# Attention through memory slots and a routed feed-forward layer: new layout and new issuer for the softmax factors, pieces of 16 tokens

## The chip, the cores and the metric

The kernel runs on one core of one Trainium2 chip. The metric is device time in microseconds (us) of one execution. Shown are the median of three runs of the kernel before and one profiled execution of it.

## The reference

Two blocks follow each other. The inputs q, k and v have the shape 8 batches x 8 heads x 576 tokens x 64; phi has 32 memory slots in the last dimension instead of 64.

```python
a = exp(phi - max(phi, slots)); a = a / (sum(a, slots) + 1e-9)
k_m = einsum('bhsm,bhsd->bhmd', a, k)
v_m = einsum('bhsm,bhsd->bhmd', a, v)
attn = softmax(q @ k_m^T / sqrt(64))          # over the 32 slots
x = (attn @ v_m) -> (8, 576, 512)
scores = x @ w_gate                           # one number a token
for each batch: the 128 tokens of the largest score get
    x + sigmoid(score) * (relu(x @ w1) @ w2)  # w1 512x1024, w2 1024x512
```

All is float32. Which tokens are chosen depends on small differences of scores, which is why the kernel computes the softmax factors and the sums over tokens with split numbers.

## The kernel before, in words

A group is one batch and four of its eight heads; there are 16 groups (`groups`, L110). The program is written as Python generators that a loop (L753 to L786) advances by hand. One pass of the loop is a turn. In each turn the softmaxes advance one step, the splitting of v advances in some turns (L763), the sums over tokens advance 7, 10 or 12 steps of two tokens each (`steps`, L730), the attention of up to two batches advances one step each, and the feed-forward products advance two. This fixes the program order on every engine; each engine then runs its own instructions in that order, and waits for others only through semaphores.

The parts that matter here:

- `softmax` and `keys` (L187, L306) work on one group. Two chains, `ch` 0 and 1, alternate until groups 0 to 7 are done; then chain 0 alone does groups 8 to 15. A group takes about ten steps: some 25 passes of VectorE (DVE) over 128 x 576 elements, with ScalarE (ACT) passes between them. `keys` then transposes the factors on TensorE (PE), copies them to `aS`, splits them into `hi` (12 bits cleared) and `lo` (the remainder), stores both to the DRAM array `aparts` (L323 to L327), and multiplies `aS` with k to get the group's k_m, which two ACT copies put into `kbd` (L336). The buffers of `lo` and `hi` are named "low" and "big"; the next group of the chain writes "lo" and "big" again at L212 and L213. `load_k` (L228) asks for the group's k.
- `split_v` (L284) loads a part of v (L291), splits it on DVE (L294, L296), and stores both parts to the DRAM array `vparts`, each twice (L298). Its pool `vio2` has one buffer in the second half of the program.
- `all_sums` (L355) computes v_m for a set of two batches at a time, so there are four sets of four groups. For each piece of T = 18 tokens `load_rows` (L341) issues five transfers on SyncE's queue (SP): one of `v_rows` and four of `a_rows`, one for each head. Every transfer puts rows of (batch, group, part) on partitions, with the tokens of the piece behind each other in the row, so that one matmul of 32 rows (L382) sums the products of the split parts for one token and one group. There are three buffers of each (`k % 3`), and 576 / 18 = 32 pieces a set. The pieces of a set are not asked for before all four groups were finished 5 turns ago (L367).
- `attention` (L676) centres k_m and v_m, computes `scores`, asks for the q of the next batch (L683, in two halves, two buffers), and goes on with `attend` (L527), `rank` and `gather`; `ffn` (L636) computes the products for the chosen tokens.

All loads go through SP's queue in program order: phi, k, v, q, the weights, and the rows. All stores, and the gathers, are issued by GpSimd (POOL). An issue that waits for a semaphore, for instance for a buffer that is still read, holds up every later issue of its queue.

The layouts of the two DRAM arrays (L830, L831) are

```python
vparts = (B, H // 4, 2, 2, 4, S, Dh)
aparts = (4, B, H // 4, 2, S, 32)       # head first, then batch, group, part, token, slot
```

and `aS`, `hi` and `lo` lie in SBUF as 96 partitions x (6 chunks x 128 columns), where token = chunk * 96 + partition and column = head * 32 + slot.

Of the kernel before, what the change touches and what calls it, by code (L numbers as in the profile page):

```python
# [8 lines left out]
F32 = mybir.dt.float32  # L9
# [11 lines left out]
NC = 6  # L21
# [18 lines left out]
def kernel(  # L40
# [15 lines left out]
    nc = tc.nc  # L56
    ctx.enter_context(tc.manual_schedule())
    B, S, D = out.shape
    PT = S // NC
# [4 lines left out]
    H = 2 * NPR  # L64
    Dh = D // H
    M = P // 4
    F = w1.shape[1]
    KD, KF = D // P, F // P
    SET = 2
    T = 18  # L70
    scale = 1.0 / Dh ** 0.5
    out_flat = out.rearrange("b s d -> (b s) d")

# [15 lines left out]
    vio = first.enter_context(tc.tile_pool(name="vio", bufs=2))  # L89
# [12 lines left out]
    def load_k(i, ch):  # L102
        ks[i] = exs[ch].tile([PT, NC, D // NG], F32, name="kb")
        nc.sync.dma_start(out=ks[i], in_=k[groups[i]])

    def load_q(b, j):
        qs[b, j] = step.tile([P, NPR, S // 2], F32, name="qb")
        nc.sync.dma_start(out=qs[b, j], in_=qT[b, :, :, j * (S // 2):(j + 1) * (S // 2)])
# [78 lines left out]
    def softmax(i, ch):  # L187
# [37 lines left out]
            tt(out=val, in0=end, in1=low, op=ALU.add)  # L225

        yield
        load_k(i, ch)  # L228
        near(den, -0.2734375, ends[0])
        dh = t("dh", I16)  # L230
        act(dh, den, FINE)
# [16 lines left out]
        tt(out=low, in0=low, in1=lo, op=ALU.add)  # L248
        stt(out=num, in0=big, scalar=UP, in1=low, op0=ALU.add, op1=ALU.add)
        yield  # L250

        dl, p = t("lo"), t("big")
        stt(out=dl, in0=den, scalar=FINE, in1=dh, op0=ALU.mult, op1=ALU.subtract)
# [30 lines left out]
    def split_v(some, pool, cuts):  # L284

        n = 4 * S * Dh // P
        for b, g in some:
            for x0 in range(0, n, n // cuts):
                x = slice(x0, x0 + n // cuts)
                vb = pool.tile([P, n // cuts], F32, name="vb")  # L290
                nc.sync.dma_start(out=vb, in_=v[b, g, :, x])  # L291
                yield
                hi = pool.tile([P, n // cuts], F32, name="vhi")
                nc.vector.tensor_single_scalar(hi.bitcast(I32), vb.bitcast(I32), -4096,  # L294
                                               op=ALU.bitwise_and)
                nc.vector.tensor_sub(vb, vb, hi)  # L296
                for vp, src in enumerate((vb, hi)):
                    nc.gpsimd.dma_start(  # L298
                        out=vparts[b, g, :, vp].rearrange("w r s d -> w (r s d)")
                                               .rearrange("w (p x) -> p w x", p=P)[:, :, x],  # L300
                        in_=src.unsqueeze(1).to_broadcast([P, 2, n // cuts]))
                yield
# [3 lines left out]
    def keys(i, ch):  # L306
        ex, (b, g) = exs[ch], groups[i]
        a = soft.pop(i)
        kb = ks.pop(i)
        aS = ex.tile([P, NC * P], F32, name="lo")[:PT].rearrange("p (c m) -> p c m", m=P)  # L310
        for c0 in range(0, NC, 3):
            tp = bank([PT, 3, P])
            for c in range(3):
                nc.tensor.transpose(out=tp[:, c], in_=a[:, (c0 + c) * PT:(c0 + c + 1) * PT],  # L314
                                    identity=ident)
            nc.scalar.activation(aS[:, c0:c0 + 3], tp, AF.Copy)  # L316
        yield
        hi = ex.tile([P, NC * P], F32, name="big")[:PT].rearrange("p (c m) -> p c m", m=P)
        lo = ex.tile([P, NC * P], F32, name="low")[:PT].rearrange("p (c m) -> p c m", m=P)
        nc.vector.tensor_single_scalar(hi.bitcast(I32), aS.bitcast(I32), -4096,  # L320
                                       op=ALU.bitwise_and)
        nc.vector.tensor_sub(lo, aS, hi)  # L322
        for part, src in enumerate((lo, hi)):  # L323
            for h in range(4):
                nc.gpsimd.dma_start(  # L325
                    out=aparts[h, b, g, part].rearrange("(c p) m -> p c m", p=PT),
                    in_=src[:, :, h * M:(h + 1) * M])  # L327
        km = bank([P, 2, 2 * M])
        for rr in range(2):
            for c in range(NC):  # L330
                nc.tensor.matmul(out=km[:, rr], lhsT=kb[:, c, rr * P:(rr + 1) * P],  # L331
                                 rhs=aS[:, c, rr * 2 * M:(rr + 1) * 2 * M],
                                 start=(c == 0), stop=(c == NC - 1))
        for u in range(2):
            part = slice(u * Dh, (u + 1) * Dh)
            nc.scalar.activation(kbd[b][part, 2 * g:2 * g + 2, u * M:(u + 1) * M],  # L336
                                 km[part, :, u * M:(u + 1) * M], AF.Copy)

    accs = [accp.tile([P, 512], F32, name=f"acc{i}") for i in range(2 * SET)]

    def load_rows(k, st, ch):  # L341

        some = slice(st * SET, (st + 1) * SET)
        nc.sync.dma_start(
            out=v_rows[k % 3][0::2].rearrange("p s d -> p (s d)").bitcast(F32),
            in_=vparts[some].rearrange("b g t w r s d -> (b g t w r) (s d)")
                [:, ch * T * Dh:(ch + 1) * T * Dh])
        for h in range(4):
            src = aparts[h, some].rearrange("b g t s m -> (b g t) (s m)")
            src = src[:, ch * T * M:(ch + 1) * T * M]  # L350
            nc.sync.dma_start(  # L351
                out=a_rows[k % 3][2 * h::8, h].rearrange("p s m -> p (s m)").bitcast(F32),
                in_=src.unsqueeze(1).to_broadcast([4 * SET, 2, T * M]))

    def all_sums():  # L355
# [7 lines left out]
        def load_some(end):  # L363
            while len(loaded) < min(end, len(pieces)):
                st, ch = pieces[len(loaded)]

                if not all(turn >= made.get(i, turn) + 5  # L367
                           for i in range(st * SET * NG, (st + 1) * SET * NG)):
                    break
                load_rows(len(loaded), st, ch)  # L370
                loaded.append(turn)
# [155 lines left out]
    def attend(b, general):  # L527
        eT, tg = eTs[b % 2], tgs[b % 3]
        row, rest = mean[b]
        for c0 in range(0, NT, 2):  # L530
# [5 lines left out]
                                     rhs=heads_of, start=True, stop=True)  # L536
            if working:
                yield
            rd = step.tile([P, 2, H], F32, name="rd")[:, :cols]
            nc.vector.tensor_scalar(out=rd.rearrange("p c (g h) -> p c g h", g=2), in0=den,  # L540
                                    scalar1=float(M), scalar2=1e-9, op0=ALU.add, op1=ALU.add)
# [134 lines left out]
    def attention(b, general=False):  # L676
        yield from centre(b)
        yield
        yield from (scores_less_max if general else scores)(b)
        for j in range(2):  # L680
            yield
            if not general and b + 1 < B:
                load_q(b + 1, j)  # L683
        yield from attend(b, general)
        yield
        yield from rank(b)
        for t in range(nt):
            yield from gather(b, t)
            chosen.append((b, t))
# [62 lines left out]
    turn = 0  # L752
    while True:  # L753
# [6 lines left out]
        if working and next(working[0], working) is working:  # L760
            finish(working[1])
            working.clear()
        if working and turn % (2 if attend_all else 4) == 1:  # L763
            next(working[1], None)
        for _ in range(steps()):
            next(sums, None)
        if attend_all is None and set(order[1]) <= set(made):
# [4 lines left out]
                ctx.enter_context(tc.tile_pool(name=name, bufs=2 - (name == "one"),  # L772
                                               reuse_waits="tile"))
                for name in ("step", "work", "one"))
            vio = ctx.enter_context(tc.tile_pool(name="vio2", bufs=1, reuse_waits="tile"))
            working[1] = split_v(groups[two + 1:], vio, 2)
            for j in range(2):
                load_q(0, j)
# [58 lines left out]
```

## Time and profile before

| what | value |
|---|---|
| median of three runs | 908.98 us (899.76 to 917.44) |
| profiled execution, its own time | 899.93 us |
| its span | 898.1 us, 25253 instructions |
| mean granted TensorE clock | 0.822 |
| PE busy (PE weight loads) | 584.2 us (427.7) |
| DVE busy | 611.5 us |
| ACT busy | 295.3 us |
| POOL busy | 234.9 us |
| stores of `aparts`, issued by POOL | 64 of `lo`, 46.9 us; 64 of `hi`, 46.5 us; 72 KB each |
| stores of `vparts`, issued by POOL | 23 and 23, 16.9 and 16.6 us; 1152 or 576 KB each |
| row loads, issued by SP | 128 of `v_rows`, 288 KB each; 512 of `a_rows`, 36 KB each |

Line 2 of the page gives the busy share in 40 slices of 22.5 us, in tenths:

```profile
PE   0122322556764646695847889867889989888794
DVE  4899888857874765779789685979845333537820
ACT  3434434324441513332433624343331310332130
POOL 7033311330220432151423314232511010112200
DMA  6367936876857786788554778664256566123300
```

The first sum over tokens starts at 142.6 us and the last at 772.8 us; the last store of softmax factors is issued at 649.7 us. A line of a list of waits reads: the engine and the line that waited, what it waited for, us in total, how often, and the longest. "SPq" is SyncE's queue of transfers. A line of a list in order of time has the start, the duration, the engine, the line, the operation, destination <- source and how many of them.

### The profile page before, as it was taken

To read this page: it belongs to the slowest core of one execution; us is meant where nothing else is said; L and a number is where in the kernel's file an instruction comes from. 1 tells how busy PE (TensorE), PEld (TensorE's weight loads), DVE (VectorE), ACT (ScalarE), POOL (GpSimd) and SP (SyncE) were. 2 spreads that over 40 slices of the span, in tenths; PEclk is the share of its full clock that TensorE was granted. 3 is DMA by queue.
4 is the path that set the end of the run, shared out by engine and by line. 5 is a ranking of instruction groups with operands and counts; after the bars stand their busy time and mean duration, and the time that the engine had idled before them with its cause. 6 is when DMAs were issued, how large, how long until landed. Compare 5 with 4: busy or idle time off the path is not lost. (4 is left out here: it accounts for less than half of the span.)

```text
span 898.1 us, 25253 instructions
## 1 busy us (share of the span) xinstructions
PE 584.2 (65%) x10738; PEld 427.7 (48%) x10738; DVE 611.5 (68%) x1117; ACT 295.3 (33%) x578; POOL 234.9 (26%) x349
## 2 busy tenths in 40 slices
PE   0122322556764646695847889867889989888794
PEld 0012222456653535574714557555556577544441
DVE  4899888857874765779789685979845333537820
ACT  3434434324441513332433624343331310332130
POOL 7033311330220432151423314232511010112200
PEclk9999999757585776886667979985899977989597
DMA  6367936876857786788554778664256566123300
GB/s 169 144 198 271 312 124 204 274 250 176 253 154 241 231 259 186 254 289 254 181 186 139 221 210 256 201 191 138 71 171 195 181 202 204 58 77 117 117 25 15
DMA packets 61944, 166.10 MB, mean 185 GB/s; under 512 B 11136, under 2 KB 21376, under 8 KB 61824
## 3 DMA queue, kind: packets, MB, share of 16 engines
q1 hardware_dynamic: 40096, 94.14, 34.8%
q0 software_dynamic: 21728, 70.27, 23.7%
q8 instruction: 87, 1.43, 0.7%
q14 instruction: 33, 0.27, 0.1%
HBM read 96.21 MB, written 68.16 MB: 183 GB/s over the span
## 5 line engine op out<-in xcount | busy, mean ns | idle before, releaser
L382 PE MATMUL acc<-a_rows,v_rows 32*64 32x128 f32 x9216 | 214.3, 253 | 127.8 <-DMA a_rows<-aparts 121.4
L382 PEld LDWEIGHTS acc<-a_rows,v_rows 32*64 32x64 f32 x9216 | 193.5, 162 | 170.4 <-issue 83.0
L314 PE MATMUL bank<-ident,num 128*96 128x128 f32 x96 | 21.3, 386 | 104.4 <-DVE num L279 99.4
L331 PE MATMUL bank<-lo,kb 96*128 96x64 f32 x384 | 64.5, 345 | 20.0 <-ACT lo L316 20.0
L331 PEld LDWEIGHTS bank<-lo,kb 96*128 96x128 f32 x384 | 62.7, 257 | 25.5 <-ACT lo L316 22.4
L325 POOL DMA_DIRECT2D aparts<-low x64 | 46.9, 740 | 104.8 <-DVE low L322 89.7
L298 POOL DMA_DIRECT2D vparts<-vb x23 | 16.9, 735 | 217.8 <-DVE vb L296 217.8
L654 PE MATMUL bank<-w_sb,xeT 128*128 128x512 f32 x128 | 69.8, 679 | 4.9 <-ACT xeT L645 3.2
L314 PEld LDWEIGHTS bank<-ident,num 128*96 128x96 f32 x96 | 15.4, 178 | 108.8 <-issue 88.4
L664 PE MATMUL bank<-w_sb,hT 128*128 128x512 f32 x128 | 60.8, 609 | 0.0
L548 PE MATMUL bank<-vbd,eT 128*128 128x256 f32 x160 | 58.3, 499 | 0.0
L552 DVE TENSOR_TENSOR xj<-bank,rd 128x512 f32<-128x512 f32 x40 | 27.5, 688 | 32.9 <-PE bank L548 32.4
L601 DVE SCALAR_TENSOR_TENSOR cmp<-row,tg,wide 128x576 bf16<-128x576 f32 x40 | 32.5, 814 | 24.0 <-ACT row L587 23.1
L325 POOL DMA_DIRECT2D aparts<-big x64 | 46.5, 734 | 3.8 <-DMA vparts<-vhi 3.7
L548 PEld LDWEIGHTS bank<-vbd,eT 128*128 128x128 f32 x160 | 34.1, 236 | 16.0 <-issue 12.1
L654 PEld LDWEIGHTS bank<-w_sb,xeT 128*128 128x128 f32 x128 | 25.3, 215 | 30.6 <-issue 22.1
L275 ACT ACTIVATE vh<-num,sm 128x576 f16<-128x576 f32 x16 | 12.4, 776 | 78.2 <-DVE sm L270 63.1
L555 POOL TENSOR_TENSOR xj<-xj,mean 128x1024 f32<-128x1024 f32 (+1 forms) x11 | 23.6, 2147 | 49.5 <-DVE xj L552 41.6
L479 DVE SCALAR_TENSOR_TENSOR eT<-es,th 128x288 f32<-128x288 f32 x32 | 14.4, 450 | 31.9 <-ACT th L477 31.9
L664 PEld LDWEIGHTS bank<-w_sb,hT 128*128 128x128 f32 x128 | 22.5, 189 | 25.9 <-issue 24.4
L336 ACT ACTIVATE kbd<-bank 64x64 f32<-64x64 f32 x32 | 7.0, 218 | 83.5 <-PE bank L331 83.3
L560 POOL DMA_DIRECT2D out<-xj x24 | 16.3, 678 | 66.8 <-DVE xj L555 63.8
(149 smaller groups left out, 1155.8 us busy)
## 6 DMA issues: line engine op xcount, KB each, us to landing
v_rows<-vparts SPq DMA_DIRECT2D x128, 288.0 KB
a_rows<-aparts SPq DMA_DIRECT2D x512, 36.0 KB
vparts<-vb POOLq DMA_DIRECT2D x9, 1152.0 KB, 5.5
vparts<-vhi POOLq DMA_DIRECT2D x9, 1152.0 KB, 8.7
kb<-in_k SPq DMA_DIRECT2D x16, 576.0 KB
qb<-in_qT SPq DMA_DIRECT2D x16, 576.0 KB
out<-xj POOLq DMA_DIRECT2D x16, 512.0 KB, 4.1
xs<-xj POOLq DMA_DIRECT2D x16, 512.0 KB, 4.3
```

Of the source, the lines that this page charges most:

```text
L298: nc.gpsimd.dma_start(out=vparts[b, g, :, vp].rearrange("w r s d -> w (r s d)") .rearrange("w (p x) -> p w x", p=P)[:, :, x], in_=src.unsq ...
L314: nc.tensor.transpose(out=tp[:, c], in_=a[:, (c0 + c) * PT:(c0 + c + 1) * PT], identity=ident)
L325: nc.gpsimd.dma_start(out=aparts[h, b, g, part].rearrange("(c p) m -> p c m", p=PT), in_=src[:, :, h * M:(h + 1) * M])
L331: nc.tensor.matmul(out=km[:, rr], lhsT=kb[:, c, rr * P:(rr + 1) * P], rhs=aS[:, c, rr * 2 * M:(rr + 1) * 2 * M], start=(c == 0), stop=(c = ...
L382: nc.tensor.matmul(out=accs[i][:Dh, :P].rearrange("p (h m) -> p h m", m=M), lhsT=vr[p, s], rhs=ar[p, :, s], start=(ch == 0 and s == 0), st ...
L548: nc.tensor.matmul(out=o[:, g * 4 * Dh:(g + 1) * 4 * Dh], lhsT=eT[:, g, (c0 + c) * P:(c0 + c + 1) * P], rhs=vbd[b % 3][:, g], start=False, ...
L552: nc.vector.tensor_mul(x[:, c].rearrange("p (h d) -> p h d", d=Dh), o.rearrange("p (h d) -> p h d", d=Dh), rd[:, c].unsqueeze(2).to_broadc ...
L555: (nc.gpsimd if working else nc.vector).tensor_add(x, x, row.unsqueeze(1).to_broadcast([P, cols, D]))
L560: nc.gpsimd.dma_start(out=out[b, c0 * P:c0 * P + (cols - 1) * P + n].rearrange("(c p) d -> p c d", p=n), in_=x[:n])
L601: nc.vector.scalar_tensor_tensor(out=cmp, in0=row, scalar=g, in1=wide[:, off:off + S], op0=ALU.is_equal, op1=ALU.mult, accum_out=equal[:, ...
L654: nc.tensor.matmul(out=ps[:n], lhsT=xeT[:, d, :n], rhs=w1_sb[:, d, f0:f0 + 512], start=(d == 0), stop=(d == KD - 1))
L664: nc.tensor.matmul(out=ps[:n], lhsT=hT[:, f, :n], rhs=w2_sb[:, f], start=(f == 0), stop=(f == KF - 1))
```

## The change

T becomes 16, so that a set has 36 pieces, and `aparts` gets the layout (batch, group, part, chunk, head, 96 tokens, slot). In it 16 tokens of one head lie behind each other, since 16 divides 96. The eight stores a group by POOL become two by ACT, one for each part, behind the k_m copies. The stores of v's parts move from POOL to ACT too, one step after DVE's subtraction. The smaller row buffers leave room for a second buffer in `vio2`. `load_k` moves one step later in `softmax`, `load_q` from `attention` into the first round of `attend`. The pieces of a set may be asked for 4 turns after its groups instead of 5, and `split_v`, which now has three steps a part instead of two, advances in one turn of three (before: four) and later in two of three (before: one of two).

```diff
--- before.py
+++ after.py
@@ -67,7 +67,8 @@
     F = w1.shape[1]
     KD, KF = D // P, F // P
     SET = 2
-    T = 18
+    T = 16
+    assert PT % T == 0
     scale = 1.0 / Dh ** 0.5
     out_flat = out.rearrange("b s d -> (b s) d")
 
@@ -225,7 +226,6 @@
             tt(out=val, in0=end, in1=low, op=ALU.add)
 
         yield
-        load_k(i, ch)
         near(den, -0.2734375, ends[0])
         dh = t("dh", I16)
         act(dh, den, FINE)
@@ -248,6 +248,7 @@
         tt(out=low, in0=low, in1=lo, op=ALU.add)
         stt(out=num, in0=big, scalar=UP, in1=low, op0=ALU.add, op1=ALU.add)
         yield
+        load_k(i, ch)
 
         dl, p = t("lo"), t("big")
         stt(out=dl, in0=den, scalar=FINE, in1=dh, op0=ALU.mult, op1=ALU.subtract)
@@ -294,8 +295,9 @@
                 nc.vector.tensor_single_scalar(hi.bitcast(I32), vb.bitcast(I32), -4096,
                                                op=ALU.bitwise_and)
                 nc.vector.tensor_sub(vb, vb, hi)
+                yield
                 for vp, src in enumerate((vb, hi)):
-                    nc.gpsimd.dma_start(
+                    nc.scalar.dma_start(
                         out=vparts[b, g, :, vp].rearrange("w r s d -> w (r s d)")
                                                .rearrange("w (p x) -> p w x", p=P)[:, :, x],
                         in_=src.unsqueeze(1).to_broadcast([P, 2, n // cuts]))
@@ -320,11 +322,6 @@
         nc.vector.tensor_single_scalar(hi.bitcast(I32), aS.bitcast(I32), -4096,
                                        op=ALU.bitwise_and)
         nc.vector.tensor_sub(lo, aS, hi)
-        for part, src in enumerate((lo, hi)):
-            for h in range(4):
-                nc.gpsimd.dma_start(
-                    out=aparts[h, b, g, part].rearrange("(c p) m -> p c m", p=PT),
-                    in_=src[:, :, h * M:(h + 1) * M])
         km = bank([P, 2, 2 * M])
         for rr in range(2):
             for c in range(NC):
@@ -335,6 +332,10 @@
             part = slice(u * Dh, (u + 1) * Dh)
             nc.scalar.activation(kbd[b][part, 2 * g:2 * g + 2, u * M:(u + 1) * M],
                                  km[part, :, u * M:(u + 1) * M], AF.Copy)
+        for part, src in enumerate((lo, hi)):
+            nc.scalar.dma_start(
+                out=aparts[b, g, part].rearrange("c h p m -> p (c h) m"),
+                in_=src.rearrange("p c (h m) -> p (c h) m", m=M))
 
     accs = [accp.tile([P, 512], F32, name=f"acc{i}") for i in range(2 * SET)]
 
@@ -346,8 +347,8 @@
             in_=vparts[some].rearrange("b g t w r s d -> (b g t w r) (s d)")
                 [:, ch * T * Dh:(ch + 1) * T * Dh])
         for h in range(4):
-            src = aparts[h, some].rearrange("b g t s m -> (b g t) (s m)")
-            src = src[:, ch * T * M:(ch + 1) * T * M]
+            src = aparts[some, :, :, ch * T // PT, h].rearrange("b g t p m -> (b g t) (p m)")
+            src = src[:, ch * T % PT * M:(ch * T % PT + T) * M]
             nc.sync.dma_start(
                 out=a_rows[k % 3][2 * h::8, h].rearrange("p s m -> p (s m)").bitcast(F32),
                 in_=src.unsqueeze(1).to_broadcast([4 * SET, 2, T * M]))
@@ -364,7 +365,7 @@
             while len(loaded) < min(end, len(pieces)):
                 st, ch = pieces[len(loaded)]
 
-                if not all(turn >= made.get(i, turn) + 5
+                if not all(turn >= made.get(i, turn) + 4
                            for i in range(st * SET * NG, (st + 1) * SET * NG)):
                     break
                 load_rows(len(loaded), st, ch)
@@ -536,6 +537,9 @@
                                      rhs=heads_of, start=True, stop=True)
             if working:
                 yield
+            if c0 == 0 and not general and b + 1 < B:
+                for j in range(2):
+                    load_q(b + 1, j)
             rd = step.tile([P, 2, H], F32, name="rd")[:, :cols]
             nc.vector.tensor_scalar(out=rd.rearrange("p c (g h) -> p c g h", g=2), in0=den,
                                     scalar1=float(M), scalar2=1e-9, op0=ALU.add, op1=ALU.add)
@@ -679,8 +683,6 @@
         yield from (scores_less_max if general else scores)(b)
         for j in range(2):
             yield
-            if not general and b + 1 < B:
-                load_q(b + 1, j)
         yield from attend(b, general)
         yield
         yield from rank(b)
@@ -760,7 +762,7 @@
         if working and next(working[0], working) is working:
             finish(working[1])
             working.clear()
-        if working and turn % (2 if attend_all else 4) == 1:
+        if working and (turn % 3 if attend_all else turn % 3 == 1):
             next(working[1], None)
         for _ in range(steps()):
             next(sums, None)
@@ -772,7 +774,7 @@
                 ctx.enter_context(tc.tile_pool(name=name, bufs=2 - (name == "one"),
                                                reuse_waits="tile"))
                 for name in ("step", "work", "one"))
-            vio = ctx.enter_context(tc.tile_pool(name="vio2", bufs=1, reuse_waits="tile"))
+            vio = ctx.enter_context(tc.tile_pool(name="vio2", bufs=2, reuse_waits="tile"))
             working[1] = split_v(groups[two + 1:], vio, 2)
             for j in range(2):
                 load_q(0, j)
@@ -828,7 +830,7 @@
                                    kind="ExternalInput").ap())
     out = nc.dram_tensor("out", (B, S, H * Dh), F32, kind="ExternalOutput").ap()
     vparts = nc.dram_tensor("vparts", (B, H // 4, 2, 2, 4, S, Dh), F32, kind="Internal").ap()
-    aparts = nc.dram_tensor("aparts", (4, B, H // 4, 2, S, phi.shape[3]), F32, kind="Internal").ap()
+    aparts = nc.dram_tensor("aparts", (B, H // 4, 2, NC, 4, PT, phi.shape[3]), F32, kind="Internal").ap()
     xs = [nc.dram_tensor(f"xs{b}", (S, H * Dh), F32, kind="Internal").ap() for b in range(B)]
     with tile.TileContext(nc) as tc:
         tile_abc_attention__then__mixture_of_depths_kernel(tc, *args, out, xs, vparts, aparts, int(moe_capacity))
```

## The prediction

> **What bounds the kernel now.** I read the page's slices first, then the waits of the whole span, then the SP queue in order of time, and last the busy times of stretches cut where the row loads start and stop. The program splits into five stretches: softmaxes alone (0 to 138 us), the sums of sets 0 and 1 (138 to 420), a pause (420 to 460), the sums of set 2 beside softmaxes and attention (460 to 650, the last 40 of them idle for the sums), the sums of set 3 (650 to 773), and the rest (773 to 898).
>
> ```profile
> core 0: us, PE busy (x) PEld busy (x) DVE busy (x) ACT busy (x) POOL busy (x), PEclk, DMA share, GB/s
> 138.00:266.00 128.00, 72.87 (x2136) 66.89 (x2136) 100.48 (x159) 48.29 (x78) 29.28 (x42) 0.73 0.73 225
> 266.00:420.00 154.00, 96.48 (x2664) 81.16 (x2668) 105.03 (x192) 46.82 (x90) 43.44 (x59) 0.72 0.76 238
> 460.00:611.00 151.00, 116.53 (x2481) 81.05 (x2483) 120.69 (x223) 58.61 (x115) 49.43 (x62) 0.86 0.68 206
> 651.00:773.00 122.00, 113.32 (x2550) 79.51 (x2546) 49.99 (x105) 22.81 (x56) 15.25 (x25) 0.89 0.61 186
> ```
>
> These lines come from one table of stretches each. From 138 to 420 no compute engine is full: DVE has 205.5 of 282 us, PE 169. From 460 on DVE (120.7 of 151) and then PE (113.3 of 122) are near their limit. So 138 to 420 is bound by something else. The waits of PE between 200 and 300 us and the SP queue in order of time name it:
>
> ```profile
> PE acc L382 <- DMA a_rows<-aparts: 32.4, 13, 8.6
> ```
>
> ```profile
> 211.87 0.50 SPq L344 DMA_DIRECT2D v_rows<-vparts  x1
> 212.41 2.45 SPq L351 DMA_DIRECT2D a_rows<-aparts  x4
> 214.96 0.50 SPq L344 DMA_DIRECT2D v_rows<-vparts  x1
> 215.51 2.44 SPq L351 DMA_DIRECT2D a_rows<-aparts  x4
> 218.05 0.50 SPq L344 DMA_DIRECT2D v_rows<-vparts  x1
> 218.60 2.45 SPq L351 DMA_DIRECT2D a_rows<-aparts  x4
> 221.14 0.50 SPq L344 DMA_DIRECT2D v_rows<-vparts  x1
> 221.69 4.99 SPq L351 DMA_DIRECT2D a_rows<-aparts  x4
> ```
>
> SP issues without a pause: one piece of 18 tokens takes 3.09 us from start to start, five issues and nothing else, and PE waits for what they bring. Adding all SP lines from 137.5 to 420.3 gives 245.6 us of issuing in 282.8: 257 a_rows issues took 186.2 us (148.8 at the usual 579 ns) and 63 v_rows issues 43.8 (31.6 at 502 ns). So 50 us are stretched issues, like the 4.99 above. The remaining 37 us are mostly gaps of 0.05 to 0.1 us between issues, and some 20 us of SP waiting for a free row buffer (L344 on PE acc). I take this stretch as bound by SP's issuing. PE works in order, so its stalls hold the transposes of the softmaxes back too.
>
> The queue's own waits over the whole span are what the change aims at:
>
> ```profile
> SPq L291 <- DMA vparts<-vb: 105.0, 6, 28.3
> ...
> SPq L351 <- DMA aparts<-big: 67.1, 6, 38.9
> SPq L344 <- PE acc L382: 62.7, 37, 11.6
> SPq L108 <- PE bank L490: 29.7, 2, 25.2
> SPq L104 <- PE bank L331: 21.8, 4, 13.7
> ```
>
> Asked by stretches of 100 us, they lie badly for a gain: of the 105.0 us of L291, 53.4 fall before 100 us (no rows are loaded then), 17.4 in 100 to 200 and 34.2 in 420 to 460; the 25.2 of L108 fall after the last row load, and only 4.6 of L104's between 138 and 420.
>
> **The Trainium skill.** "Perfetto Trace Analysis", section "DMA Instruction — HWDGE (DVE, Sync)", says that the block that generates descriptors is shared by the two issuing sequencers and locked for one of them at a time, and that the profiled time of an issue includes the wait for the lock. Here only SP issues that way, so the trace cannot confirm the sharing; that issue time grows from 0.58 to 2.9 us at worst agrees that more than decoding is in it. "DMA: Bandwidth & Descriptors", section "Issuing engines are not separate DMA queues", says that transfers started by any engine run on the same 16 engines, so that another issuer saves sequencer time only. The trace agrees in so far as SP's long issues start beside POOL's large stores: 221.69 follows the two vparts stores at 221.12 and 221.83, 144.34 those at 143.01 and 143.71.
>
> **The change part by part.** The sum is against the profiled execution, 899.9 us (span 898.1); the median of the runs shown is 909.0, so 9 us are added at the end.
>
> 1. *Pieces of 16.* 576/16 = 36 pieces a set instead of 32; each is still five SP issues, of the same forms with shorter rows, so 3.09 us undisturbed. Sets 0 and 1: 8 more pieces, 8 x 3.09 = +25 us, all of it on the bound. Set 3 (650 to 773): +12.4 us of issuing; SP has 122.6 - 104.7 = 18 us free there, about 9 of them gaps that cannot be filled, so +4. Set 2 (460 to 611): 150.6 - 114.4 = 36 us free, 26 after gaps, which covers +12.4 (it would cost that whole without the slack); +2 for more PE stalls. Bytes are unchanged. Together +31.
>
> 2. *Factors stored by ACT.* POOL loses 128 issues (46.9 + 46.5 us) and 46 for v (16.9 + 16.6). ACT gains 32 + 46. ACT's issue price is not in the trace. A store is now 96 x 24 = 2304 pieces of 128 bytes. Lower bound: SP's cheapest issue, 0.33 us. Upper: POOL gives off 576 such pieces each 0.74 us without a growing delay to landing (3.5 and 4.3 us), so the DMA engines take them at least that fast: 4 x 0.73 = 2.9 us. Nearest rows: qb, 512 rows in 0.59 us, and w2, 1024 rows in 1.16: 1.14 ns a row, 2.6 us for 2304. I take 2.6. For v's parts (256 rows) 0.5 us. ACT thus gets 32 x 2.6 + 46 x 0.5 = 106 us on top of 295; it has room over the span. What matters is whether those issues keep SP from its own. From 138 to 420 there are 7 groups and 12 v pieces: 14 x 2.6 + 24 x 0.5 = 48 us of ACT issuing. If the block is locked, up to +48 us; if not, 0. Part falls where SP waits for a buffer or is stretched by busy DMA engines anyway, so I take +15. Set 2's stretch: 4 groups, 5 v pieces, 26 us against 14 of slack left: 0 to +12, I take +4.
>
> 3. *Order on ACT.* The store now stands behind the kbd copies (L336), so it waits for nothing itself. Behind it in ACT's queue stand the next group's activations and the attention's es and th; each is held 5.2 us at most. The next group's lo and big (L212, L213) must wait until the store has read them: before, ACT waited 0.2 us for this. Issue 5.2 plus landing 4 against two turns of some 4.8 us: 0 to 3 us a group, 16 groups; I take +5 in all. v's parts get a yield between DVE's subtraction and the issue, so ACT shouldn't wait for DVE there.
>
> 4. *Waits taken from SP.* Second vio2 buffer: the 21 us block at 438.6 to 460.0 ends earlier, so set 2 starts up to 13 us earlier (its last factors were issued by 442.7 and landed some 4 us later). But set 2 ends at 611 and set 3's rows wait until 650.4 for the last softmax, so that is mostly hidden; it moves some PE work ahead: -5. k one step later: -4 (the 4.6 us above). q later: L108's 25.2 us have no row loads behind them, 0; q now comes in attend, about one turn before the next batch's scores instead of two or three, a danger of -0/+5, taken as 0. One turn less after a softmax (5 to 4): at sets 0 and 3 SP already stands waiting for factors (26.3 and 38.9 us), so 0.
>
> 5. *POOL freed.* POOL's addition (L555) no longer stands behind 5.8 us of issues; DVE waited for it 6.7 us in all: -4. v's slower pace (a piece per 9 turns for 8, then 4.5 for 4) is still ahead of the sums: 0.
>
> Sum: 31 + 15 + 4 + 5 - 5 - 4 - 4 = +42: 942 us, by the median 951. Since the free bounds of 2 and 3 reach further down than I put them, I forecast 947.
>
> **Rivals.**
>
> *A, faster: the stretch goes away.* The 50 us of stretched issues between 138 and 420 come when POOL throws two stores of up to 1152 KB into the DMA engines within 1.4 us. Issued by ACT and a step later, they may be served in turn with the rows. Without the stretch and without contention: 899.9 + 31 - 13 - 50 = 868, 877 by the median. It decides from the point where more than 31 - 13 = 18 us of the 50 are saved, and beats 2% from 36. For it: the coincidences at 144 and 221 us. Against: the bytes and the DMA engines are the same.
>
> *B, no change: the stores cost SP nothing*, and the earlier start of set 2 is worth its whole 13 us: 899.9 + 31 - 21 = 910, 919 by the median. For it: the lock shows in no line. Against: nothing then explains a gain beyond that.
>
> *C, much slower: the lock holds in full*, and lo and big wait 2 us a group: 899.9 + 31 + 48 + 12 + 32 - 13 = 1010, 1019 by the median. For it: the skill's wording and SP's 87% use. Against: ACT has idle time, and the 26 us pieces of stage 460 to 611 may fall in pauses.
>
> **How the numbers follow.** Chances: the forecast 0.48 (its own range 927 to 975), A 0.27 (865 to 891), B 0.17 (891 to 927), C 0.08 (975 to 1025). Faster by over 2%, which is about what a measurement can tell from no change, is A: 0.27; within 2% is B: 0.17; slower is the forecast and C: 0.56. The range leaves out A's lower end and C: 873 to 978.
>
> **What would show it.** Right: v_rows x144 and a_rows x576 at about 502 and 579 ns, a piece at 3.09 us; sets 0 and 1 taking over 300 us from the first a_rows to the last; PE's wait for a_rows well above 121 us; ACT's aparts issues near 2.6 us. Wrong: row issues much shorter than 579 ns; the stretched part gone while ACT stores; ACT's issues near 0.4 us; or a softmax stage (to the last aparts store, now at 650) that is shorter than before.

## The result, and the profile after

The changed kernel takes 1013.2 us (median of 4 runs, 1011.7 to 1014.5) against 905.9 for the kernel before in the same comparison: a ratio of 1.121, 95% interval 1.113 to 1.129. It is slower, and by more than the range of the prediction (873 to 978) allowed. The profiled execution took 1011.9 us (span 1010.1), 112 us more than that of before.

These stretches of after answer to those shown of before, cut by the same rule: from the first to the last issue of `a_rows` of a set, and for set 3 to the last sum. Sets 0 and 1 now run from 145 to 493, set 2 from 519 to 699, set 3 from 745 to 883:

```profile
core 0: us, PE busy (x) PEld busy (x) DVE busy (x) ACT busy (x) POOL busy (x), PEclk, DMA share, GB/s
145.00:312.00 167.00, 82.33 (x2168) 76.19 (x2168) 102.15 (x161) 49.48 (x80) 0.41 (x2) 0.62 0.61 187
312.00:493.00 181.00, 108.72 (x2684) 90.72 (x2685) 107.15 (x196) 46.11 (x89) 13.82 (x20) 0.63 0.64 194
519.00:699.00 180.00, 134.06 (x2564) 92.43 (x2563) 125.12 (x234) 63.12 (x122) 28.23 (x31) 0.78 0.62 186
745.00:883.00 138.00, 118.38 (x2553) 81.14 (x2549) 50.02 (x105) 22.83 (x56) 14.63 (x23) 0.86 0.52 162
```

Sets 0 and 1 take 348 us instead of 282, with nearly the same DVE work (209 us, before 205.5). Set 2 takes 180 instead of 150 (its first `a_rows` was issued at 461 before), set 3 takes 138 instead of 122. These are 112 us. What lies around them adds up to nothing: the row loads start 7 us later, the pause ahead of set 2 is 15 us shorter, the one ahead of set 3 is 6 us longer, and what follows the last sum is 2 us longer (127.7 us, before 125.3). So the loss lies in the stretches in which rows are loaded. The bytes are the same and the share of the DMA engines' time in use fell, so the engines are no fuller than before. PE's wait between 200 and 300 us:

```profile
PE acc L383 <- DMA a_rows<-aparts: 55.7, 13, 16.1
```

It was 32.4 us; over the span it is 203.7 (before 121.4). The granted clock fell too, from 0.822 to 0.767, and PE's busy time in sets 0 and 1 rose by 22 us. Had a slower PE held SP back, SP's wait for a row buffer that PE still reads would have grown; it is 62.0 us, before 62.7. But no run holds the clock fixed, so a part of the time, in set 3 above all (PE 118.4 us, before 113.3), may be the clock's.

The waits of SP's queue over the span hold what is new:

```profile
SPq L352 <- DMA aparts<-big: 92.5, 6, 46.2
...
SPq L345 <- PE acc L383: 62.0, 35, 13.8
SPq L292 <- DMA vparts<-vb: 42.3, 4, 14.8
SPq L105 <- PE bank L328: 41.6, 3, 16.7
SPq L109 <- PE bank L491: 30.1, 2, 25.7
SPq L352 <- DMA vparts<-vb: 28.9, 5, 13.5
SPq L345 <- DMA vparts<-vb: 26.7, 5, 11.4
SPq L352 <- DMA vparts<-vhi: 16.8, 11, 3.8
```

The last three lines are loads of rows (L345, L352) that wait for stores of v's parts. With a line of 3.0 us for L345 and vparts<-vhi they sum to 75.4 us. The kernel before has 1.3 us of it (its L351 is L352 here):

```profile
SPq L351 <- DMA vparts<-vb: 0.7, 1, 0.7
SPq L351 <- DMA vparts<-vhi: 0.6, 1, 0.6
```

L352 reads `aparts` and needs nothing from `vparts`. Two lists in order of time show one such place, SP's queue first, ACT's issues second:

```profile
161.82 2.45 SPq L352 DMA_DIRECT2D a_rows<-aparts  x4
164.37 0.50 SPq L345 DMA_DIRECT2D v_rows<-vparts  x1
170.59 4.08 SPq L352 DMA_DIRECT2D a_rows<-aparts  x4
174.76 0.50 SPq L345 DMA_DIRECT2D v_rows<-vparts  x1
```

```profile
164.72 0.37 ACTq L300 DMA_DIRECT2D vparts<-vb  x1
165.12 0.53 ACTq L300 DMA_DIRECT2D vparts<-vhi  x1
171.91 0.33 ACTq L336 DMA_DIRECT2D aparts<-low  x1
172.28 2.31 ACTq L336 DMA_DIRECT2D aparts<-big  x1
```

SP stands from 164.87 to 170.59, until the store that ACT issues at 164.72 has landed. Why it must is in the program: the transfers issued by SP and by ACT take turns on eight semaphores in program order, and each waits until the last transfer on its semaphore has landed. The trace agrees: the load at 170.59 waits for the very semaphore that the store at 164.72 carries, and all 872 transfers of SP and ACT in it use the same eight. These are five consecutive transfers of SP's program; the number behind DMAHW names the semaphore, 0 to 7:

```
L352 DMACopy a_rows0_106<-aparts 16x1x512 [waits DMAHW4_49]
L352 DMACopy a_rows0_106<-aparts 16x1x512 [waits DMAHW5_49]
L352 DMACopy a_rows0_106<-aparts 16x1x512 [waits DMAHW6_49]
L345 DMACopy v_rows1_104<-vparts 64x1024 [waits DMAHW1_49,PE_49]
L352 DMACopy a_rows1_107<-aparts 16x1x512 [waits DMAHW2_49]
```

Between 6 and 1, the numbers 7 and 0 have gone to two transfers of ACT. In the kernel before only SP's transfers took numbers of this set, and the next one waited for SP's own transfer eight back, mostly landed; POOL's have another eight. Now SP, which runs far ahead of the compute engines, can pass a transfer of ACT's by seven places and no further. ACT reaches it in its own order, behind DVE.

### The profile page after: what moved, and what is told of

Its sections match the earlier page's. It is cut to its first block, busy times and chain, and to the rows that moved or that the text cites. A ratio compares the mean times of both kernels' runs of the same rounds, so it can differ in the third digit from the quotient of the medians.

```text
span 1010.1 us, 25145 instructions
## 1 busy us (share of the span) xinstructions
PE 624.2 (62%) x10738; PEld 456.6 (45%) x10738; DVE 610.9 (60%) x1116; ACT 295.2 (29%) x578; POOL 108.6 (11%) x176
## 3 DMA queue, kind: packets, MB, share of 16 engines
q10 hardware_dynamic: 86752, 47.19, 16.4%
## 5 line engine op out<-in xcount | busy, mean ns | idle before, releaser
L383 PE MATMUL acc<-a_rows,v_rows 32*64 32x128 f32 x9216 | 228.1, 263 | 209.4 <-DMA a_rows<-aparts 203.7
L383 PEld LDWEIGHTS acc<-a_rows,v_rows 32*64 32x64 f32 x9216 | 206.0, 172 | 255.6 <-issue 152.3
L316 PE MATMUL bank<-ident,num 128*96 128x128 f32 x96 | 21.7, 391 | 105.9 <-DVE num L280 105.9
L328 PE MATMUL bank<-lo,kb 96*128 96x64 f32 x384 | 68.7, 360 | 19.7 <-ACT lo L318 17.9
L658 PE MATMUL bank<-w_sb,xeT 128*128 128x512 f32 x128 | 75.6, 728 | 5.1 <-ACT xeT L649 4.3
L328 PEld LDWEIGHTS bank<-lo,kb 96*128 96x128 f32 x384 | 66.9, 272 | 24.1 <-ACT lo L318 19.8
L322 DVE TENSOR_SCALAR big<-lo 96x768 int32<-96x768 int32 x16 | 8.8, 552 | 55.4 <-ACT lo L318 55.4
L245 DVE SCALAR_TENSOR_TENSOR lo<-num,vh 128x576 f32<-128x576 f32 x16 | 12.1, 755 | 41.0 <-ACT vh L182 41.0
L205 DVE SCALAR_TENSOR_TENSOR ph<-q,ph 128x576 f32<-128x576 int16 x32 | 25.4, 795 | 17.6 <-ACT q L182 17.1
L318 ACT ACTIVATE lo<-bank 96x384 f32<-96x384 f32 x32 | 14.5, 483 | 65.8 <-PE bank L316 65.7
L536 PEld LDWEIGHTS bank<-heads_of,eT 128*128 128x128 f32 x160 | 29.8, 270 | 5.1 <-issue 3.0
```

The source lines that it names most:

```text
L205: stt(out=r, in0=q, scalar=-ln2, in1=r, op0=ALU.mult, op1=ALU.add)
L383: nc.tensor.matmul(out=accs[i][:Dh, :P].rearrange("p (h m) -> p h m", m=M), lhsT=vr[p, s], rhs=ar[p, :, s], start=(ch == 0 and s == 0), st ...
L536: nc.tensor.matmul(out=den[:, c, g], lhsT=eT[:, g, (c0 + c) * P:(c0 + c + 1) * P], rhs=heads_of, start=True, stop=True)
L658: nc.tensor.matmul(out=ps[:n], lhsT=xeT[:, d, :n], rhs=w1_sb[:, d, f0:f0 + 512], start=(d == 0), stop=(d == KD - 1))
```

## The experiments

Three theories were set against each other. Theory 1: the shared semaphores tie SP to ACT. Theory 2: the busy path, that is the bytes, the 128-byte pieces and the long issues on the way through ACT. Theory 3: the additional issues of T = 16. Six of the kernels make a path from before to after, on which each step is one edit or one group of edits. Times are medians, and "before" was 905.9 to 911.4 us in the comparisons. The intervals reach about 4 to 7 us to each side, so a step of a few us cannot be told from nothing.

| kernel | us | ratio to before, 95% interval | PE waits for a_rows, us |
|---|---|---|---|
| before | 909 | | 121.4 |
| T = 16 alone | 948.2 | 1.043, 1.038 to 1.048 | 142.6 |
| and the edits of order | 935.3 | 1.029, 1.022 to 1.037 | 151.6 |
| and the new layout, two stores by POOL | 953.3 | 1.045, 1.038 to 1.052 | 166.3 |
| and the second vio2 buffer | 954.2 | 1.051, 1.046 to 1.055 | 166.1 |
| and v's parts stored by ACT | 995.2 | 1.098, 1.092 to 1.103 | 194.4 |
| and the factors stored by ACT (after) | 1013.2 | 1.121, 1.113 to 1.129 | 203.7 |

The steps are +39, -13, +18, +1, +41 and +18 us.

**T = 16 alone.**

```diff
-    T = 18
+    T = 16
```

> The kernel before with T = 16 and nothing else. Theory 1 (shared slots: SP's row loads wait for ACT's late stores, because the transfers that SP and ACT issue take turns on eight semaphores): T = 16 is only a part, 31 us as in the forecast, so 930 to 940 us. Theory 2 (busy path: ACT's stores of 128-byte pieces load the DMA engines and stretch SP's issues): the same, 930 to 940. Theory 3 (SP's issue time for the 16 additional pieces is the main cost and was underrated): 970 us or more.

Measured: 948.2 us, +38 over 910.3 in its comparison. A bit more than the term of the forecast (31), far from theory 3's 970. Its profile is of a run of 953.7 us, 54 above the profile of before. There sets 0 and 1 take 24 us more, as the forecast had it (25), but set 2 takes 11 more (forecast 2) and set 3 takes 145 us instead of 122, where the forecast had 4 more.

**Stores by POOL, in the new layout.** The changed kernel with this edit at both places, v's parts and the factors:

```diff
-                    nc.scalar.dma_start(
+                    nc.gpsimd.dma_start(
```

> The changed kernel, but all stores of factors and of v's parts issued by POOL again, in the new layout and at the new places. Theory 1: POOL's transfers have semaphores of their own, so the waits of SP for stores go and the time falls to 930 to 945 us. Theory 2: falls as far, if POOL's stores are packed into fewer packets as before. Theory 3: stays at 990 us or more.

Measured: 954.2 us, ratio 1.051 (1.046 to 1.055): the issuer is worth 59 us, and theory 3 falls as the main cause. Theory 1 had 945 at most; it left out the merging of the stores, which costs 17 us (below). The place and the size of the stores are as in the changed kernel, and POOL's transfers take none of the eight semaphores; SP's row loads wait 2.4 us for vparts stores.

**One of the two kinds of store by POOL.** The same edit for v's parts only, and for the factors only.

> The changed kernel, but v's parts stored by POOL again; the factors are still stored by ACT. Theory 1: in the changed kernel SP waits 75 us for vparts stores that its loads don't need, against few for the factors beyond the 92 us that are mostly a true dependence; without them 950 to 975 us. Theory 2: the 128-byte pieces remain, so 995 us or more.

> The changed kernel, but the factors stored by POOL, in two transfers a group; v's parts are still stored by ACT. Theory 1: the waits for vparts stores remain, 975 us or more. Theory 2: the 128-byte pieces leave the hardware path, 950 us or less.

Measured: 973.4 us (1.063 to 1.078) with v's parts back on POOL, 995.2 (1.092 to 1.103) with the factors back on POOL. Both as theory 1 had it; v's parts are the dearer half.

**Small transfers by ACT.** The kernel before, with `note()` behind each store of v's parts and twice behind the k_m copies:

```diff
+    def note():
+        nc.scalar.dma_start(out=notes[len(noted)], in_=ident[:16, :64])
+        noted.append(1)
...
+                    note()
```

> The kernel before, plus 78 small transfers (16 rows of 256 bytes from a constant to a scratch array) issued by ACT where the changed kernel's ACT issues stand: two behind each group's k_m copies, two behind each v part. They wait for no data, carry next to no bytes and few descriptors, and nobody reads them. Theory 1 (shared slots): each takes one of the eight semaphores that SP's loads use in turn, so SP stands until ACT has come to it: 945 to 970 us, with SP waits for these transfers in the trace. Theory 2 (busy path: bytes, packets and long issues): 915 us or less.

Measured: 929.3 us, ratio 1.022 (1.014 to 1.030). SP's row loads wait 18.1 us for the small transfers. Theory 1 is seen nearly without bytes, but smaller than expected (945 to 970); theory 2 expected 915 or less. It stayed open what carries the rest.

**Long pieces.** The changed kernel with each store of 96 pieces of 3072 bytes; it leaves out that the factors must lie in the order in which the row loads read them. Number, size and addresses of the row loads stay the same:

```diff
-                out=aparts[b, g, part].rearrange("c h p m -> p (c h) m"),
-                in_=src.rearrange("p c (h m) -> p (c h) m", m=M))
+                out=aparts[b, g, part].rearrange("c h p m -> (c h p m)").rearrange("(p x) -> p x", p=PT),
+                in_=src.rearrange("p c k -> p (c k)"))
```

> The changed kernel, but each factor store writes 96 pieces of 3072 bytes instead of 2304 of 128: the factors are laid down partition by partition, which is not the order in which the row loads read them, so this run leaves the right order of the factors out. Theory 1: the number of stores and what they wait for are the same, so 1000 us or more. Theory 2: the cost of 128-byte pieces goes, about the 18 us between the run with v by ACT and the changed kernel, or more: 995 us or less.

Measured: 987.2 us, ratio 1.085 (1.078 to 1.091), 26 us below the changed kernel. Here theory 2 was right: for the factors it is the pieces that cost. With long pieces the kernel is even 8 us below the one with the factors stored by POOL (995.2). ACT's issues of the two stores, min, median and max in ns, first in the changed kernel, then with long pieces:

```profile
L336 ACTq DMA_DIRECT2D aparts<-low x16: 311/329/340, 48.4 to 739.4; - x16
L336 ACTq DMA_DIRECT2D aparts<-big x16: 1986/2252/4621, 48.7 to 739.7; - x16
```

```profile
L336 ACTq DMA_DIRECT2D aparts<-low x16: 310/328/341, 48.3 to 710.4; - x16
L336 ACTq DMA_DIRECT2D aparts<-big x16: 437/440/711, 48.7 to 710.8; - x16
```

The first store is issued in 0.33 us in both; the second takes 2.25 us in the changed kernel, against 0.44. The Trainium skill, "DMA: Bandwidth & Descriptors", section "Specifications", has 512 bytes as the least piece for full rate; these runs agree in direction: for the same bytes ACT's stores take 13.0% of the DMA engines' time over a span of 984.6 us with long pieces, against 16.4% over 1010.1, which is 128 against 166 us.

How the pieces cost time is seen on ACT itself. The word "issue" stands for idle time in which an engine waited for nothing that the profile shows. In the changed kernel each of these times follows directly on a store's issue by ACT; first the changed kernel, then long pieces:

```profile
ACT dh L182 <- issue: 20.2, 6, 4.8
ACT ph L200 <- issue: 6.8, 2, 4.7
```

```profile
ACT ph L200 <- issue: 3.1, 3, 2.0
ACT dh L182 <- issue: 1.1, 2, 0.6
```

L182 and L200 are activations of the softmaxes, which stand behind the store issues in ACT's program order. With long pieces the first `a_rows` is issued at 134.6 us instead of 145.0, so 10 of the 26 us are gained before any row is loaded. How the rest divides between these waits and the busier DMA engines was not tried apart. The row loads still wait 53 and 17 us for v's stores here, so the pieces and the shared semaphores are two separate causes.

**The edits of order alone**, on the kernel before, T = 18, stores by POOL: `load_k` and `load_q` later, 4 turns for 5, the additional yield and the pace of `split_v`.

> The kernel before with only the edits of order: k and q asked for later, pieces 4 turns after a group, the additional step in splitting v and its new pace. T stays 18, stores stay with POOL, one vio2 buffer. From the run with POOL's stores less the run with T = 16 alone (954 less 948) I expect 905 to 920 us; if the edits of order cost by themselves and the second buffer and the new layout paid them back, 925 or more.

Measured: 898.9 us, ratio 0.987 (0.976 to 0.998). This part of the change seems to gain: the interval hardly leaves 1 out, but the same edits also gain 13 us at T = 16 (948.2 to 935.3). It is the only version here whose time lies below both kernels.

**Fewer and larger pieces, and the reverse.** To test that the count of issues is what T costs, T = 24 with two row buffers (`k % 2`, `load_some(k + 2)`) and T = 12 with four (`k % 4`, `load_some(k + 4)`), otherwise the kernel before:

```diff
-    T = 18
+    T = 24
```

> The kernel before with T = 24 and two row buffers instead of three: 24 pieces a set, so five issues for 24 tokens. If SP's issue time bounds the stretch from 138 to 420 us, 40 issues fewer a set give back what T = 16 cost: 870 to 890 us. If the number of buffers matters as much (48 tokens in flight instead of 54, and only one piece ahead), 906 us or more.

```diff
-    T = 18
+    T = 12
```

> The kernel before with T = 12 and four row buffers: the same 48 tokens in flight as with T = 16 and three, but 48 pieces a set instead of 36. If the count of SP's issues is what T = 16 pays for, 24 more pieces in sets 0 and 1 at 3.09 us cost 74 us over the run with T = 16 alone, and more in the last set: 1010 us or more. If the tokens in flight are what it pays for, about as T = 16: 940 to 960 us.

Measured: T = 24 took 940.1 us, ratio 1.031 (1.024 to 1.038), and T = 12 took 1032.5, ratio 1.136 (1.128 to 1.144). T = 12 keeps the 48 tokens in flight of T = 16 and pays 84 us more, for its greater number of pieces. T = 24 saves issues, but with two buffers SP waits for PE to free one, which with T = 18 and three buffers took 62.7 us. SP's waits of the two, T = 24 first:

```profile
SPq L344 <- PE acc L382: 207.8, 64, 18.9
```

```profile
SPq L344 <- PE acc L382: 24.5, 26, 8.9
```

So both sizes matter, and between 12 and 16 it is the count. The cost isn't where it was expected: sets 0 and 1 take 47 us more with T = 12 than with 16 (expected 74), the rest comes later.

**SP's own waits taken away.** The edits of order, with v's loads, then v's and k's, issued by POOL:

```diff
-                nc.sync.dma_start(out=vb, in_=v[b, g, :, x])
+                nc.gpsimd.dma_start(out=vb, in_=v[b, g, :, x])
```

> The edits of order at T = 18, and the loads of v issued by POOL instead of SP. Every theory that takes SP's queue for the bound from 138 to 420 us: SP loses 23 issues and 44 us of waits for vparts stores, so 880 to 892 us. If these waits are hidden, as the prediction held, 895 to 903 us.

> As the run with v's loads on POOL, and k's loads on POOL too. SP loses another 53 us of waits for a k buffer. If those waits hold row loads up, 870 to 885 us; if POOL, which waits for a buffer in its turn, then delays its stores and gathers, 895 us or more.

Measured: 907.9 us, ratio 0.999 (0.996 to 1.002), and 911.7, ratio 1.002 (0.999 to 1.004). The waits leave SP's queue and nothing is gained. In the first run SP's wait for a row buffer grew from 63.7 to 86.8 us and that for a k buffer from 53.4 to 69.1: SP is ahead, and arrives earlier at the next wait. Both even lose the 10 us of the edits of order. A candidate, not shown to be the cause: in each run one row load stood longer for a store of v by POOL, 12.1 and 31.4 us, against 2.3 with the edits of order alone.

**Layout, merging, buffer.** On T = 16 with the edits of order (935.3 us):

```diff
-            vio = ctx.enter_context(tc.tile_pool(name="vio2", bufs=1, reuse_waits="tile"))
+            vio = ctx.enter_context(tc.tile_pool(name="vio2", bufs=2, reuse_waits="tile"))
```

> The kernel before with T = 16 and the edits of order, stores by POOL in the old layout, one vio2 buffer. The edits of order gained 10 us at T = 18; on top of T = 16 alone (948) that gives 935 to 942 us. The run with POOL's stores in the new layout and two vio2 buffers took 954; so if this one is near 938, the new layout or the second buffer cost some 15 us; if it is near 954, they cost nothing and the edits of order gain only at T = 18.

> T = 16 and the edits of order (935 us), plus the second vio2 buffer and nothing else. If the second buffer costs (v's stores come in closer pairs and run ahead of what is needed): 948 to 956 us. If the new layout costs: 930 to 940 us; the prediction had the second buffer as a gain of 5 us.

The other three keep one buffer and have the new layout: with two stores behind the k_m copies, with eight at the old place, and with two at the old place.

```diff
-                    out=aparts[h, b, g, part].rearrange("(c p) m -> p c m", p=PT),
+                    out=aparts[b, g, part, :, h].rearrange("c p m -> p c m"),
```

> T = 16 and the edits of order (935 us), plus the new layout with two stores a group by POOL, behind the k_m copies, and one vio2 buffer. If the new layout or place of the stores costs (landing took 6.7 us instead of 3.5): 948 to 956 us. If the second buffer costs: 930 to 940 us.

> T = 16 and the edits of order (935 us), with the new layout of the factors in DRAM, but still eight stores a group by POOL, at the old place. If the row loads suffer from where the rows now stand: 948 to 956 us. If merging or moving the stores costs: 930 to 940 us.

> The same with two stores a group by POOL, at the old place, ahead of the k_m matmuls. If the merging costs (landing 6.7 us instead of 3.5): 948 to 956 us, with the run of eight stores near 935. If the place behind the k_m copies costs: near 935 us, as nothing but the place then parts it from the run at 953.

Measured: second buffer 937.8 us (ratio 1.018 to 1.034), the new layout with two stores 953.3, with eight stores 937.3 (1.027 to 1.038), with two stores at the old place 954.0 (1.041 to 1.054). So the second buffer, the layout and the place cost nothing that can be measured, and merging eight stores into two costs 17 us. POOL issues the two within 2.4 us instead of 5.8, and they take longer to land; first the eight, then the two:

```profile
DMA to landing us min/median/max: 2.5/3.8/5.8
```

```profile
DMA to landing us min/median/max: 5.5/6.8/10.0
```

From the issue of the first to the landing of the last it is about 9 us in both (5.9 + 3.8, 2.4 + 6.8), so the factors aren't later. But SP's row issues beside them are. Counted is how much the row issues that start within 11 us of a group's first factor store last beyond their usual 579 ns (`a_rows`) and 503 ns (`v_rows`): 9 to 10 us in all in the three kernels of T = 16 with eight stores by POOL, 29 to 30 us in the three with two. These 20 us are close to the 17; what makes an issue longer beside a denser burst, the trace doesn't say.

**v's parts by ACT at T = 18**, on the edits of order, once in full and once with two small transfers by ACT in the same places while POOL stores v.

> The edits of order at T = 18 (899 us), with v's parts stored by ACT and nothing else. Both theories: 930 to 945 us, as the same step cost 41 us at T = 16; below 915 us the step would cost only together with T = 16.

> The edits of order at T = 18, v's parts stored by POOL, plus two small ACT transfers (16 rows of 256 bytes from a constant) where the run with v by ACT stores them. Theory 1 (shared semaphores): most of what v by ACT costs, less the longer landing of a large store, so 915 to 930 us. Theory 2 (large stores on the hardware path): 905 us or less.

Measured: 950.2 us, ratio 1.040 (1.033 to 1.048), and 933.3, ratio 1.022 (1.014 to 1.031), against 898.9 without either. The step costs 51 us here, and small transfers that carry next to nothing and wait for no data cost 34 of them. The row loads' waits, v by ACT first (with 3.6 us more in a line not shown), then the small transfers:

```profile
SPq L345 <- DMA vparts<-vb: 29.2, 4, 8.6
SPq L352 <- DMA vparts<-vb: 16.8, 3, 9.0
...
SPq L352 <- DMA vparts<-vhi: 13.6, 10, 3.0
```

```profile
SPq L353 <- DMA notes<-ident: 31.8, 4, 11.8
...
SPq L360 <- DMA notes<-ident: 17.6, 7, 11.0
```

63 us of waiting for 51 us of time, 49 for 34: theory 1 carries about two thirds of v's step, at T = 18. Both expectations were a little too low (945 and 930 at most). The rest is what a large store adds by landing later, or by its bytes; these two weren't parted.

## Why the prediction was wrong, by its own steps

The direction was right, and for pieces of 16 tokens the reason was too. What failed is the price of the new issuer.

- What bounds the kernel: right. Sets 0 and 1 hang on SP's queue (T = 12 and T = 16), and the waits that the change takes from SP are worth nothing, as the prediction held: with v's loads off SP's queue the time stays at the kernel before. The signs named for the forecast came (144 and 576 row issues at 503 and 579 ns, sets 0 and 1 over 300 us, PE's wait at 203.7 us), but for ACT's issues of `aparts`: one of each pair was near 2.6 us, the other near the 0.4 us that was named as a sign of being wrong.
- Step 1, pieces of 16: the mechanism was right for sets 0 and 1, the term +31 measured +38. Mis-sized was set 3, "+4": 23 us longer in the profile of T = 16 alone. SP had time to spare there: its wait for a row buffer in set 3 rose from 10.6 to 21.7 us. PE waits 19.5 us for `a_rows` (before 7.1), and its busy time is 122.7 us (before 113.3) at a granted clock of 0.85 (before 0.89). Whether the fewer tokens in flight, the count of pieces or the clock did this was not tried apart.
- Step 2, factors and v stored by ACT: this is the step that failed. It asked "whether those issues keep SP from its own" through a lock on the block that generates descriptors, as the Trainium skill, "Perfetto Trace Analysis", section "DMA Instruction — HWDGE (DVE, Sync)", describes it, and took +15 and +4 for both kinds of store together. Measured: +41 for v and +18 for the factors. No such lock keeps SP out: its `a_rows` issues last 574 ns at least and 579 in the median, as before, and 2060 at most (before 2935), and twelve of them start and end inside an issue of ACT of over 1 us, three of these at 574 to 575 ns. Together these twelve are 4.7 us longer than at 579 ns each. What keeps SP back is not ACT's issuing but its lateness, through the eight semaphores; the prediction counted issues by their length and never asked what a transfer is ordered behind. For the factors the 128-byte pieces came on top. The price of 2.6 us an issue was twice too high: it holds for a pair (0.33 and 2.25).
- The merging of eight stores into two was not priced at all: +17 us by the run with POOL.
- Step 3, order on ACT, +5: the mechanism came, larger. It named 5.2 us at most for which ACT's next activations stand behind a store; ACT stood up to 4.8 us, 27 us in all at L182 and L200. Once, for 5.6 us, it waited for a factor store to be done; the prediction had 0 to 3 us a group for that.
- Steps 4 and 5: the second buffer was put at -5 and gives nothing that can be measured. The edits of order were put at -4 and give 10 to 13 us; which of them gains wasn't tried apart. DVE's wait for POOL's addition fell from 6.7 to 2.5 us, as step 5 had it; its worth in time was not measured.
- Rival A expected SP's stretched issues to go, and named v's stores on ACT as a gain. Its 50 us were read from lines that hold four issues with the gaps between them; issue by issue they are 37 us between 138 and 420. In the changed kernel they are 25 us in sets 0 and 1, against 50 with the same stores by POOL. So this relief is real, but the waits for v's stores outweigh it.
- Rival C gave 1019 us, next to the measured time, but by the lock in full, which is not in the trace, and by 32 us of waits for lo and big, of which ACT shows 5.6. That it came so near is luck.

The path of six edits goes from 909 to 1013.2 us and puts a number to each step. Open stay why SP's issues last longer beside merged stores, what parts the last 17 us of v's step, and what the lower clock adds.

## What to carry to other kernels

Before a transfer moves to another queue, look up what the program orders it behind: transfers of two engines that take turns on one set of semaphores tie the engine that runs ahead to the one that lags, however little they carry. A queue that works almost without a pause pays for most of each additional issue, so a smaller piece is dear there even where bytes stay the same. A long issue also costs the engine that makes it: what stands behind it in program order waits. Waits that a queue spends ahead of its users are hidden; taking them away moves SP to its next wait.

## What the runs showed of the hardware that was not expected

- ACT issues a store of 2304 pieces of 128 bytes in 0.33 us, and a second one right behind it in 2.25 us; with 96 pieces of 3072 bytes the second takes 0.44 us.
- For the same 128-byte pieces the number of packets says little of the time: ACT's factor stores ran as 74240 packets in 6.6% of the DMA time of a 975.8 us span (64 us); with POOL's stores of the same data, the software queue's share falls by the same 64 us when they leave it (23.9% of 960.9 us against 17.0% of 975.8), with about 3000 packets fewer on it.
- Two stores issued within 2.4 us cost 17 us more over the kernel than eight of the same data within 5.8 us, and SP's row issues beside them last 20 us longer in all.
- SP can issue a transfer in its usual 574 ns in the middle of a 2.3 us issue by ACT.
